# Full-height idle matmuls, a split first batch and a reordered load queue in a fused attention and SwiGLU kernel

## The chip, the cores and the metric

The kernel runs on one core of a Trainium2 chip. The metric is device time in microseconds; the median of several executions stands for a kernel. The profile is of one execution, and its own time is given beside its span.

The core's engines are named as the profile names them: PE (matmul) and PEld (its weight loads), DVE (vector), ACT (scalar), POOL (here mostly the issuer of load DMAs) and SP (the issuer of store DMAs and of DMA transposes).

## The reference

```python
batch, n_heads, seq, head_dim = (8, 12, 448, 64)
n_tokens, d_model, d_ff = (3584, 768, 1536)

scores = q @ k.T / sqrt(64)                 # per batch and head
attn = maximum(scores, 0) ** 2 / 448        # squared ReLU in place of a softmax
x = (attn @ v), heads side by side          # 3584 tokens x 768

xn = x / sqrt(mean(x * x) + 1e-6) * rms_g
out = (silu(xn @ w_gate) * (xn @ w_val)) @ w_out
```

Inputs and output are float32; inside, the kernel works in bf16 with float32 sums.

## The kernel before

**Tiling.** Heads go in pairs (six pairs, two to a "visit", so three visits to a sub-batch). Batch 0 is cut into two halves of 224 query columns, `a0` and `a1` (`subs[0]`, `subs[1]`); each later batch is one piece of 448. For each piece the kernel makes

- transposes of q and k into `qkT` (PSUM tile `psT`), by the PE for batches 0 and 1, by DMA after that;
- scores in units (`psS`, and `psR` for the last 64 keys), then ReLU and square into `r` (L656/L658 and L664), on DVE and ACT, some squares on POOL in batch 1;
- attention times v, three visits (`psAV`), copied to `xT` and squared to `x`;
- the sum of squares by a matmul against ones (`psSS`), then Ln, Exp and a table load on ACT and six scalings on DVE into `xn`;
- the feed-forward: gate (`psg`) and value (`psv`) by blocks f of 128 features, twelve in all, evacuated as `sil` on ACT and `hT` on DVE; then the output projection (`psO`), three column pieces to a tile of 128 tokens.

Most matmuls use 64 rows of the array. Two of them, one on the low and one on the high 64 rows, run side by side: the low half works one segment while the high half works the segment before it.

**The order is written out ahead of time.** The program places every instruction by hand (`tc.manual_schedule()`). While the kernel is built, the class `Planner` steps through a model of the engines: each half of the PE has a clock `t`, each other engine a time `free`, each DMA a modelled landing. At each step it picks what the model says is ready, and that fixes the order of each engine's queue. On the chip each queue then runs strictly in that order, and an instruction waits for what it really needs.

**Idle matmuls.** While batch 0's first feed-forward segment has not begun (`warm()` returns `0 not in started`), and nothing is ready in the model for 250 ns, `choose` inserts a `filler` (L293). It calls `fill()` (L1212), which issues one matmul of `ones_bf` against `busy_bf` (zeros), on the low 64 rows, 224 columns, into a free PSUM bank (`psB`, L1220). The model books 380 ns for it up to `WARM = 4500` ns and 96 ns after.

**Loads.** All are issued by POOL, in the order of L1104 to L1123, through `issue` (L405). A load waits until the one eight places before it has landed (`ahead=8`). `issue` also holds the model's price of a load on POOL (700 ns), its rate and its lag. The order is: q, k and v of batch 0 in three groups of heads (the first two query chunks of q), the other two query chunks of q, weights for blocks 0 to 8 in pairs (one `wg`, one `wv` load each), k and q of batch 1 for its first six heads, weights for blocks 8 to 12, v of batch 1, the rest of k and q of batch 1, and `wo` in two loads. For batches 2 and later, `load_later` issues loads when a batch's attention is done.

**The feed-forward's order.** `pl.stream` holds the segments. For batch 0 it has blocks 0 to 8 in pairs for `a0`, the same for `a1`, then blocks 8 to 12 one by one for `a0` and `a1` together (448 columns). The planner may take any of the first `WINDOW = 8` entries that is ready.

Of the kernel before, what the change touches and what calls it, by code (L numbers as in the profile page):

```python
# [13 lines left out]
NCH = 4  # L14
U = 7
UH = 4
# [38 lines left out]
class Planner:  # L55
# [1 line left out]


    SEM, PSUM, HAND, SW = 50.0, 210.0, 200.0, 95.0
    SLOW, WARM = 700.0, 4500.0  # L60

    def __init__(self, nc, tc, banks, wide, warm):
        self.nc, self.tc, self.banks, self.wide, self.warm = nc, tc, banks, wide, warm
# [227 lines left out]
        self.units.pop(0).begin()  # L291

    def filler(self):  # L293
        self.row()
        s = max(self.t)
        cost = self.fill() or 96.0
        TRACE.append((s, cost, "fil", "filler"))
        self.t = [s + cost, s + cost]
# [26 lines left out]
def kernel(  # L325
# [11 lines left out]
    nc = tc.nc  # L337
    P = nc.NUM_PARTITIONS
    B, H, S, D = q.shape
    T, DM = out.shape  # L340
    _, F = moe_w_gate.shape
    assert (T, DM) == (B * S, H * D) and 2 * D == P and S % NCH == 0 and B % 2 == 0 and S == U * D
    PC = S // NCH
    KT, FT, HP = DM // P, F // P, H // 2
# [29 lines left out]
    pl = Planner(nc, tc, banks, wide, None)  # L374
# [7 lines left out]
    low, high = slice(0, D), slice(D, P)  # L382
# [3 lines left out]
    ones_bf = const.tile([P, P], BF16, name="ones_bf", tag="ones_bf")  # L386
    nc.vector.memset(ones_bf[:], 1.0)
    busy_bf = const.tile([P, HALF], BF16, name="busy_bf", tag="busy_bf")
# [12 lines left out]
    ld, ldtok = {}, {}  # L401
    src_of = {"q": q, "k": k, "v": v}
    dma = {"t": 0.0, "landed": []}

    def issue(fn, nbytes, need=(), rate=385.0, cost=700.0, ahead=8):  # L405

        tok = Tok()
        land = dma["landed"]
        need = list(need) + (land[-ahead:][:1] if len(land) >= ahead else [])
        land.append(tok)  # L410

        def go(e):
            fn()
            end = pl.free["pool"]
            at = max(dma["t"], end + 1200.0)
            dma["t"] = at + nbytes / (rate if at > 8000.0 else 290.0)
            lag = 3200.0 if dma["t"] > 6000.0 else 1700.0
            TRACE.append((end - cost, dma["t"] + lag - end + cost, "dma", "%d" % nbytes))
            return dma["t"] + lag - end

        pl.task(-1, {"pool": cost}, go, need, tok)
        return tok

    def new_ld(nm, b):
        if (nm, b) not in ld:
            n, w = (PC, NCH) if nm == "q" else (P, UH)
            runs = nm == "v" or b < PE_T
            shape = [n, H, w * D] if runs else [n, w, H * D]
            ld[nm, b] = ldpool.tile(shape, BF16, name=nm + "b", tag=nm + "b")
            if nm == "k" and runs:  # L430
                nc.vector.memset(ld[nm, b][D:, :, (UH - 1) * D :], 0.0)
            ldtok[nm, b] = {}
        return ld[nm, b]

    def load_runs(nm, b, h0, h1, part, u0, u1, c0=0):

        t = new_ld(nm, b)
        n = PC if nm == "q" else D

        def go():  # L440
            nc.gpsimd.dma_start(
                out=t[part, h0:h1, c0 * D : (c0 + u1 - u0) * D],
                in_=src_of[nm][b, h0:h1].rearrange("h (p u) d -> p h (u d)", p=n)[:, :, u0 * D : u1 * D],
            )

        tok = issue(go, n * (h1 - h0) * (u1 - u0) * D * 4)
        for h in range(h0, h1):
            ldtok[nm, b].setdefault(h, []).append(tok)
        return tok

    def load_q(b, h0, h1, c0=0, c1=NCH):
        return load_runs("q", b, h0, h1, slice(0, PC), c0, c1, c0)

    def load_k(b, h0, h1):
        load_runs("k", b, h0, h1, low, 0, UH)
        load_runs("k", b, h0, h1, high, UH, U)

    def load_v(b, h0, h1):
        load_runs("v", b, h0, h1, low, 0, UH)
        load_runs("v", b, h0, h1, high, UH - 1, U)  # L460

    def load_later(b, need):

        for nm in ("k", "q"):
            t = new_ld(nm, b)
            n = PC if nm == "q" else D
            rows = src_of[nm][b].rearrange("h (p u) d -> p u h d", p=n)
            to = t[:].rearrange("p u (h d) -> p u h d", d=D)
            if nm == "q":
                parts = [(to[:], rows)]  # L470
            else:
                parts = [(to[low, u : u + 1], rows[:, u : u + 1]) for u in range(UH)]
                parts += [(to[high, u - UH : u - UH + 1], rows[:, u : u + 1]) for u in range(UH, U)]
            for o, i in parts:
                tok = issue(
                    lambda o=o, i=i: nc.gpsimd.dma_start(out=o, in_=i),  # L476
                    S * DM * 4 / len(parts), need, 200.0, 2300.0 if nm == "q" else 1080.0,
                )
                ldtok[nm, b].setdefault("all", []).append(tok)
        new_ld("v", b)  # L480
        for part, u0, u1 in ((low, 0, UH), (high, UH - 1, U)):
            def go(part=part, u0=u0, u1=u1):
                nc.gpsimd.dma_start(  # L483
                    out=ld["v", b][part, :, : (u1 - u0) * D],
                    in_=v[b].rearrange("h (p u) d -> p h (u d)", p=D)[:, :, u0 * D : u1 * D],
                )
            tok = issue(go, D * H * 4 * D * 4, need)
            for h in range(H):
                ldtok["v", b].setdefault(h, []).append(tok)

    wtok = {}

    def load_w(f0, f1):
        for nm, dst, src in (("g", wg_sb, moe_w_gate), ("v", wv_sb, moe_w_val)):
            def go(dst=dst, src=src):
                nc.gpsimd.dma_start(
                    out=dst[:, :, f0 * P : f1 * P],
                    in_=src.rearrange("(kt p) f -> p kt f", p=P)[:, :, f0 * P : f1 * P],
                )
            tok = issue(go, P * KT * (f1 - f0) * P * 4)  # L500
            for f in range(f0, f1):
                wtok[nm, f] = tok

    def load_wo(f0, f1):
        def go():
            nc.gpsimd.dma_start(
                out=wo_sb[:, f0:f1, :],
                in_=moe_w_out.rearrange("(fk p) m -> p fk m", p=P)[:, f0:f1, :],
            )
        tok = issue(go, P * (f1 - f0) * DM * 4)  # L510
        for f in range(f0, f1):
            wtok["o", f] = tok

# [355 lines left out]
    def finish(sub):  # L869

        b = sub.b
        if sub.q0 + sub.n == S and b + 2 < B:
            load_later(b + 2, [Tok(max(pl.t))])
            transpose_dma(b + 2)
# [227 lines left out]
    nc.sync.dma_start(out=g_sb[:], in_=moe_rms_g.rearrange("(kt p) -> p kt", p=P))  # L1102

    load_q(0, 0, 4, 0, 2)  # L1104
    load_k(0, 0, 4)
    identTok = pl.task(-1, {"pool": 550.0}, lambda e: masks.make_identity(nc, ident[:]) and None)
    load_q(0, 4, 8, 0, 2)
    load_k(0, 4, 8)
    load_v(0, 0, 4)
    load_q(0, 8, H, 0, 2)  # L1110
    load_k(0, 8, H)
    load_v(0, 4, H)
    load_q(0, 0, H, 2, 4)
    for f in range(0, 8, 2):
        load_w(f, f + 2)
    load_k(1, 0, H // 2)
    load_q(1, 0, H // 2)
    load_w(8, FT)
    load_v(1, 0, H)
    load_k(1, H // 2, H)  # L1120
    load_q(1, H // 2, H)
    load_wo(0, FT // 2)
    load_wo(FT // 2, FT)  # L1123


    a0, a1 = subs[0], subs[1]
# [28 lines left out]
    for si, sub in enumerate(subs):  # L1155
        lst = []
        for kk in range(HP // 2):
# [3 lines left out]
            else:  # L1161
                n = sub.n
# [25 lines left out]


    for sub in (a0, a1):  # L1190
        for f in range(0, 8, 2):
            pl.stream.append(ffn_seg([sub], "g", [f, f + 1]))
            pl.stream.append(ffn_seg([sub], "v", [f, f + 1]))
    for f in range(8, FT):
        pl.stream.append(ffn_seg([a0, a1], "g", [f]))
        pl.stream.append(ffn_seg([a0, a1], "v", [f]))
    for b in range(B):
        if b:
            for f in range(FT):
# [2 lines left out]
        full = S // P  # L1202
# [9 lines left out]
    def fill():  # L1212
        free = [x for x in wide + banks if x.free is not None and x.free <= max(pl.t)]
        if not free:
            return None
        bank = max(free, key=lambda x: x.free)
        if bank.fill is None:
            ps = bank.take("psB")
            bank.fill = ps[:, 0, :HALF] if bank in wide else ps[:, :HALF]
        nc.tensor.matmul(  # L1220
            out=bank.fill, lhsT=ones_bf[low, :], rhs=busy_bf[low, :], start=True, stop=True
        )
        cost = 96.0 if max(pl.t) > pl.WARM else 380.0
        bank.free = max(pl.t) + cost
        return cost

    def warm():
# [9 lines left out]
        return 0 not in started  # L1237

    pl.fill, pl.warm = fill, warm
    pl.run()  # L1240

# [29 lines left out]
```

## Time and profile before

| What | Value |
|---|---|
| median of 7 runs | 457.01 us (453.5 to 458.3) |
| profiled execution, its own time | 457.21 us |
| its span | 455.4 us |
| PE busy | 448.1 us, 98% of the span, 6091 matmuls |
| PEld busy | 310.0 us, 68% |
| DVE, ACT, POOL busy | 250.7, 246.3 and 86.8 us |
| granted PE clock in the profile | 0.999 |
| idle matmuls (`psB`) in the trace | 103, starting from 1.2 to 32.2 us |
| first feed-forward matmul (`psg`) | starts at 32.3 us |

Matmuls are pipelined and their ends are modelled, so the busy share of the PE does not say how full the array is: a lone 64-row matmul counts as busy while half the array is idle. The distance from one start to the next says more. A row of the timeline gives start, duration of the merged piece, engine, line, operation, output and inputs, count, and in brackets how long the engine had been idle and what ended that. In the chain of waits each row is start, length, engine, tile, line and count.

### The profile page before, as it was taken

The numbers are of one execution on the slowest core, as the hardware profiler recorded it, in microseconds if no ns is written. First come the engines' busy times: TensorE is split into PE (matmuls) and PEld (weight loads), VectorE is DVE, ScalarE is ACT, GpSimd is POOL, SyncE is SP. The second block draws the span as 40 slices with busy tenths as digits, with TensorE's granted clock in tenths as the row PEclk, the third lists the DMA queues.
The fourth block names the chain that finished last, engine by engine and source line by source line (L and its number), as shares of the span: only waits on it lengthen the run. The fifth ranks groups of instructions, "written<-read, shape, count | busy, mean of one in ns | idle before, by whom it ended". The sixth has DMA issues, their size and how long they took to land.

```text
span 455.4 us, 13555 instructions
## 1 busy us (share of the span) xinstructions
PE 448.1 (98%) x6091; PEld 310.0 (68%) x6091; DVE 250.7 (55%) x414; ACT 246.3 (54%) x363; POOL 86.8 (19%) x104
## 2 busy tenths in 40 slices
PE   8999999999999999999999999999999999999995
PEld 6777775776568666775668666775668666776784
DVE  2586978328763666367653666367653576242200
ACT  2595865527744667456654576456754566432221
POOL 8633635631134000510025000100000000000000
PEclk9999999999999999999999999999999999999999
DMA  9999997999999930699019920554002200020023
GB/s 97 187 197 203 203 179 93 173 158 195 136 78 203 176 50 2 78 189 154 1 14 195 195 53 1 68 136 96 1 1 71 73 1 1 1 71 1 1 77 99
DMA packets 133737, 44.52 MB, mean 98 GB/s; under 512 B 105712, under 2 KB 130096, under 8 KB 133680
## 3 DMA queue, kind: packets, MB, share of 16 engines
q0 software_dynamic: 94624, 24.39, 55.3%
q1 hardware_dynamic: 39056, 19.28, 23.1%
q8 instruction: 47, 0.77, 0.7%
q14 instruction: 10, 0.08, 0.1%
HBM read 48.76 MB, written 11.01 MB: 131 GB/s over the span
## 4 chain that ended last, share of the span: by engine, by line
PE 95%; DVE 3%; issue 0%; ACT 0%
PE psO L139 25%; PE psv L139 24%; PE psg L139 23%; PE psAV L820 9%; PE psS L713 6%; PE psB L1220 3%; PE psSS L139 2%; PE psT L579 2%; PE psR L734 1%; DVE r L656 1%; DVE xn L921 1%; DVE r L664 0%; DVE x L850 0%; PE psSS L947 0%; DVE qkT L594 0%
## 5 line engine op out<-in xcount | busy, mean ns | idle before, releaser
L139 PE MATMUL psv<-xn,wv_sb 64*128 64x448 bf16 (+1 forms) x1248 | 233.6, 335 | 0.3 <-DVE hT L996 0.2
L139 PE MATMUL psg<-xn,wg_sb 64*128 64x448 bf16 (+1 forms) x1248 | 233.3, 335 | 0.2
L139 PE MATMUL psO<-wo_sb,hT 64*128 64x256 bf16 x2016 | 135.5, 270 | 0.0
L139 PEld LDWEIGHTS <-wv_sb 64*128 64x128 bf16 x1248 | 104.5, 94 | 41.0 <-issue 3.4
L658 ACT ACTIVATE r<-psS 128x896 bf16<-128x896 f32 x123 | 111.3, 919 | 35.3 <-PE psS L713 33.7
L139 PEld LDWEIGHTS <-wg_sb 64*128 64x128 bf16 x1248 | 104.4, 94 | 36.6 <-issue 3.3
L139 PEld LDWEIGHTS <-hT 64*128 64x128 bf16 x2016 | 107.5, 94 | 24.1 <-issue 2.5
L664 DVE TENSOR_TENSOR r<-r 128x896 bf16<-128x896 bf16 (+1 forms) x167 | 98.9, 612 | 19.9 <-ACT r L658 19.3
L996 DVE TENSOR_TENSOR hT<-sil,psv 128x448 bf16<-128x448 bf16 x96 | 59.4, 619 | 60.8 <-PE psv L139 59.0
L983 ACT ACTIVATE sil<-psg 128x448 bf16<-128x448 f32 x96 | 52.1, 542 | 45.8 <-PE psg L139 42.7
L1073 ACT COPY ost<-psO 128x256 f32<-128x256 f32 x70 | 26.1, 372 | 66.9 <-PE psO L139 65.0
L713 PE MATMUL psS<-qkT 64*128 64x448 bf16 (+1 forms) x324 | 61.4, 338 | 0.4 <-DVE r L656 0.2
L820 PE MATMUL psAV<-r,vb 64*64 64x448 bf16 (+1 forms) x756 | 43.8, 340 | 0.4
L483 POOL DMA_DIRECT2D vb<-in_v_dram x12 | 9.5, 844 | 141.8 <-PE psO L139 141.8
L658 ACT ACTIVATE r<-psR 128x896 bf16<-128x896 f32 (+1 forms) x24 | 20.1, 839 | 29.0 <-PE psR L734 29.0
L476 POOL DMA_DIRECT2D kb<-in_k_dram x42 | 32.1, 857 | 18.9 <-DMA qb<-in_q_dram 15.9
L656 DVE TENSOR_SCALAR r<-psS 128x896 bf16<-128x896 f32 x21 | 22.9, 1089 | 23.2 <-PE psS L713 22.5
L847 DVE TENSOR_SCALAR xT<-psAV 128x896 bf16<-128x896 f32 (+1 forms) x20 | 20.9, 1045 | 24.0 <-PE psAV L820 24.0
L820 PEld LDWEIGHTS <-vb 64*64 64x64 bf16 x756 | 18.7, 107 | 20.4 <-PE psAV L820 8.7
L921 DVE SCALAR_TENSOR_TENSOR xn<-xT,g_sb,rstd 128x448 bf16<-128x448 bf16 (+1 forms) x54 | 31.0, 641 | 0.0
L713 PEld LDWEIGHTS <-qkT 64*128 64x128 bf16 x324 | 23.3, 96 | 9.1 <-issue 2.6
L1075 DVE COPY ost<-psO 128x256 f32<-128x256 f32 x14 | 5.9, 422 | 30.5 <-PE psO L139 30.5
(41 smaller groups left out, 206.5 us busy)
## 6 DMA issues: line engine op xcount, KB each, us to landing
vb<-in_v_dram POOLq DMA_DIRECT2D x14, 384.0 KB, 7.1
kb<-in_k_dram POOLq DMA_DIRECT2D x45, 96.0 KB, 8.1
qb<-in_q_dram POOLq DMA_DIRECT2D x6, 672.0 KB, 16.0
out_dram<-ost SPq DMA_DIRECT2D x8, 336.0 KB, 4.7
wo_sb<-in_moe_w_out_dram POOLq DMA_DIRECT2D x2, 1152.0 KB, 18.3
out_dram<-ost SPq DMA_DIRECT2D x8, 288.0 KB, 4.4
out_dram<-ost SPq DMA_DIRECT2D x8, 240.0 KB, 4.6
wg_sb<-in_moe_w_gate_dram POOLq DMA_DIRECT2D x4, 384.0 KB, 12.8
```

The source lines that it names most:

```text
L139: mm = self.nc.tensor.matmul(out=seg.bank["tile"][:, off : off + seg.w], lhsT=lhsT[prt], rhs=rhs[prt], start=(seg.first and h == 0 and i = ...
L476: lambda o=o, i=i: nc.gpsimd.dma_start(out=o, in_=i),
L656: nc.vector.tensor_relu(out=r[:, :, :w], in_=ps[:, :, :w])
L658: nc.scalar.activation(out=r[:, :, :w], in_=ps[:, :, :w], func=ACT.Relu)
L664: eng.tensor_tensor(out=r[:, :, :w], in0=r[:, :, :w], in1=r[:, :, :w], op=ALU.mult)
L713: nc.tensor.matmul(out=ps[:, hh, o : o + n], lhsT=t[prt, j, 0, c * P : (c + 1) * P], rhs=t[prt, j, 1, sub.q0 : sub.q0 + n], start=True, st ...
L820: mm = nc.tensor.matmul(out=ps[hh * D : (hh + 1) * D, jj, :n], lhsT=vt[prt, 2 * (ja + jj) + hh, u * D : (u + 1) * D], rhs=r[prt, hh, o : o ...
L847: nc.vector.tensor_scalar_mul(out=xT[at], in0=ps[:, :, :n], scalar1=inv_attn)
L921: nc.vector.scalar_tensor_tensor(out=xn[:, kt, q0 : q0 + n], in0=xTs[b, 0][:, kt, q0 : q0 + n], scalar=g_sb[:, kt : kt + 1], in1=rstd[:, q ...
L983: nc.scalar.activation(out=s[:, :m], in_=ps[:, :m], func=ACT.Silu)
L996: nc.vector.tensor_tensor(out=h[:, fbs[0] : fbs[-1] + 1, o : o + n], in0=s[:, :m].rearrange("p (f s) -> p f s", s=n), in1=ps[:, :m].rearra ...
L1073: nc.scalar.copy(out=ost[:, p * OW : (p + 1) * OW], in_=ps[:, :OW])
```

## The change

Five edits go together.

1. `fill()` issues its matmul on all 128 rows (`ones_bf[:]` against `busy_bf[:]`), and the model books 189 ns for it up to `WARM = 5500` ns, 96 after. `filler` treats it as an operation of mode "full", with the model's switch of 95 ns.
2. Batch 0's feed-forward goes by pairs of blocks for all twelve blocks, first in `a0`, then in `a1`.
3. k and q of batch 1 for the first six heads are issued ahead of the weights for blocks 4 to 8.
4. The model of a load is new: its POOL time depends on its number of runs, its rate on the length of a run, its lag on the time.
5. The load helpers are rearranged; they issue the same transfers.

```diff
-    SLOW, WARM = 700.0, 4500.0
+    SLOW, WARM = 700.0, 5500.0
...
     def filler(self):
-        self.row()
-        s = max(self.t)
+        s = max(self.t) + (self.SW if self.mode != "full" else 0.0)
+        self.mode = "full"
         cost = self.fill() or 96.0
...
-    def issue(fn, nbytes, need=(), rate=385.0, cost=700.0, ahead=8):
+    def issue(fn, nbytes, run, need=(), rate=None, ahead=8):
...
+        rate = rate or (385.0 if run > 512 else 280.0)
+        cost = 500.0 + 0.45 * nbytes / run
...
-            at = max(dma["t"], end + 1200.0)
-            dma["t"] = at + nbytes / (rate if at > 8000.0 else 290.0)
-            lag = 3200.0 if dma["t"] > 6000.0 else 1700.0
+            at = max(dma["t"], end + 1000.0)
+            dma["t"] = at + nbytes / rate
+            lag = 3200.0 if dma["t"] > 13000.0 else min(2500.0, max(850.0, 0.38 * dma["t"] - 575.0))
...
     load_q(0, 0, H, 2, 4)
-    for f in range(0, 8, 2):
-        load_w(f, f + 2)
+    load_w(0, 2)
+    load_w(2, 4)
     load_k(1, 0, H // 2)
     load_q(1, 0, H // 2)
+    load_w(4, 6)
+    load_w(6, 8)
     load_w(8, FT)
...
     for sub in (a0, a1):
-        for f in range(0, 8, 2):
+        for f in range(0, FT, 2):
             pl.stream.append(ffn_seg([sub], "g", [f, f + 1]))
             pl.stream.append(ffn_seg([sub], "v", [f, f + 1]))
-    for f in range(8, FT):
-        pl.stream.append(ffn_seg([a0, a1], "g", [f]))
-        pl.stream.append(ffn_seg([a0, a1], "v", [f]))
...
         nc.tensor.matmul(
-            out=bank.fill, lhsT=ones_bf[low, :], rhs=busy_bf[low, :], start=True, stop=True
+            out=bank.fill, lhsT=ones_bf[:], rhs=busy_bf[:], start=True, stop=True
         )
-        cost = 96.0 if max(pl.t) > pl.WARM else 380.0
+        cost = 96.0 if max(pl.t) > pl.WARM else 189.0
```

More of the change, by code (lines that the diff above doesn't have):

```diff
@@ L433, in new_ld, with landed, load_q, load_runs @@
         return ld[nm, b]
-    def load_runs(nm, b, h0, h1, part, u0, u1, c0=0):
-        t = new_ld(nm, b)
-        n = PC if nm == "q" else D
+    def landed(nm, b, h0, h1, tok):
+        for h in range(h0, h1):
+            ldtok[nm, b].setdefault(h, []).append(tok)
+    def load_q(b, h0, h1, c0=0, c1=NCH):
+        t = new_ld("q", b)
         def go():
             nc.gpsimd.dma_start(
-                out=t[part, h0:h1, c0 * D : (c0 + u1 - u0) * D],
-                in_=src_of[nm][b, h0:h1].rearrange("h (p u) d -> p h (u d)", p=n)[:, :, u0 * D : u1 * D],
-            )
[L446 to L452, printed above, removed]
+                out=t[:, h0:h1, c0 * D : c1 * D],
+                in_=q[b, h0:h1].rearrange("h (p u) d -> p h (u d)", p=PC)[:, :, c0 * D : c1 * D],
+            )
+        landed("q", b, h0, h1, issue(go, PC * (h1 - h0) * (c1 - c0) * D * 4, (c1 - c0) * D * 4))
+    def load_runs(nm, b, h0, h1, part, u0, u1, need=()):
+        t = new_ld(nm, b)
+        def go():
+            nc.gpsimd.dma_start(
+                out=t[part, h0:h1, : (u1 - u0) * D],
+                in_=src_of[nm][b, h0:h1].rearrange("h (p u) d -> p h (u d)", p=D)[:, :, u0 * D : u1 * D],
+            )
+        run = (u1 - u0) * D * 4
+        landed(nm, b, h0, h1, issue(go, D * (h1 - h0) * run, run, need))
     def load_k(b, h0, h1):
@@ L456, in load_k, with load_v @@
         load_runs("k", b, h0, h1, high, UH, U)
-    def load_v(b, h0, h1):
-        load_runs("v", b, h0, h1, low, 0, UH)
-        load_runs("v", b, h0, h1, high, UH - 1, U)
+    def load_v(b, h0, h1, need=()):
+        load_runs("v", b, h0, h1, low, 0, UH, need)
+        load_runs("v", b, h0, h1, high, UH - 1, U, need)
     def load_later(b, need):
@@ L476, in load_later @@
                     lambda o=o, i=i: nc.gpsimd.dma_start(out=o, in_=i),
-                    S * DM * 4 / len(parts), need, 200.0, 2300.0 if nm == "q" else 1080.0,
+                    S * DM * 4 // len(parts), D * 4, need, 200.0,
                 )
                 ldtok[nm, b].setdefault("all", []).append(tok)
[L480 to L489, printed above, removed]
+        load_v(b, 0, H, need)
     wtok = {}
@@ L499, in go @@
                 )
-            tok = issue(go, P * KT * (f1 - f0) * P * 4)
+            tok = issue(go, P * KT * (f1 - f0) * P * 4, (f1 - f0) * P * 4)
             for f in range(f0, f1):
@@ L509, in go @@
             )
-        tok = issue(go, P * (f1 - f0) * DM * 4)
+        tok = issue(go, P * (f1 - f0) * DM * 4, DM * 4)
         for f in range(f0, f1):
```

## Prediction

> **What bounds the kernel now.** I read the page's slices first, then counted work by stage, then followed the chain of waits through the first stage, then POOL's timeline for the landings.
>
> The slices say that the PE is busy throughout, and that its granted clock is full in all of them:
>
> ```profile
> PE   8999999999999999999999999999999999999995
> DVE  2586978328763666367653666367653576242200
> PEclk9999999999999999999999999999999999999999
> DMA  9999997999999930699019920554002200020023
> ```
>
> Both rows hide the loss. Busy counts idle matmuls (psB) and lone half-array matmuls as full. So I asked for the groups by form in stretches of 10 us, and gave each matmul the array time that it needs: columns / 2.4 GHz + 2.5 ns (the spacing at full speed in this trace: 224 columns start 96 ns apart), times the share of the array that its rows and columns take (a half for 64*128, a quarter for 64*64); a transpose 28 ns, psB nothing. For instance, of stretch 30 to 40:
>
> ```profile
> L139 PE MATMUL psg<-xn,wg_sb 64*128 64x224 bf16 x46 | 5.7, 257 | 0.0
> ```
>
> 46 x 95.8 / 2 = 2.2 us of array. Summed, the array's work is 419.3 us of the 455.4. The time lost runs up to 9.1 us at 10, 16.4 at 20, 21.6 at 30, 25.2 at 40, 26.7 at 50, 28.8 at 60, 30.2 at 90, and stays between 30.0 and 31.2 from there to 450. From 90 us on the array is full: what the first 60 us save arrives at the end undiminished; nothing after it can be gained.
>
> The chain of waits of that first stage (start, length, engine, tile):
>
> ```profile
> 7.87 0.19 PE psB L1220
> 8.05 1.37 PE psT L579 x24
> ...
> 12.22 2.05 PE psB L1220 x11
> 14.27 1.36 PE psT L579 x23
> 15.64 0.86 PE psB L1220 x4
> 16.49 0.94 PE psAV L820 x15
> ...
> 19.11 1.37 PE psT L579 x21
> 20.48 1.07 PE psS L713 x12
> 21.55 0.76 PE psB L1220 x8
> ...
> 24.94 0.71 PE psT L579 x24
> ```
>
> The same work costs two prices. Eleven psB take 2.05 us at 12.2 (187 ns each), eight take 0.76 at 21.55 (95 ns); 24 transposes take 1.37 us at 8.05 and 0.71 at 24.94. The array runs at half speed from the start to about 21.3 us, although the PEclk row shows nothing of it. And it does so under 36 psB back to back from 1.18 to 8.05 us.
>
> The queue is in order, and the planner booked 96 ns for psB that cost 187. So the PE falls behind its plan and real work waits behind psB. POOL's timeline shows by how much, since each load waits for the landing of the eighth before it:
>
> ```profile
> 10.79 0.94 POOL L441 DMA_DIRECT2D qb<-in_q_dram  x1 [0.40 <-DMA kb<-in_k_dram]
> 14.99 0.87 POOL L496 DMA_DIRECT2D wg_sb<-in_moe_w_gate_dram  x1
> 17.79 0.82 POOL L496 DMA_DIRECT2D wg_sb<-in_moe_w_gate_dram  x1 [1.10 <-DMA vb<-in_v_dram]
> 29.51 0.83 POOL L496 DMA_DIRECT2D wv_sb<-in_moe_w_val_dram  x1 [1.63 <-DMA wg_sb<-in_moe_w_gate_dram]
> 39.03 0.83 POOL L506 DMA_DIRECT2D wo_sb<-in_moe_w_out_dram  x1 [0.77 <-DMA qb<-in_q_dram]
> ```
>
> k of heads 4 to 8 is in at 10.8, its transposes run at 14.27. The issue at 14.99 waits for nothing, so k of heads 8 to 12 is in by then; its transposes run at 19.11. v is complete at 17.7, the gate weights of blocks 4 and 5 at 29.4, q of batch 1 at 39.0. DVE and ACT are not what holds this back before 21 us, but are nearly full after it (columns: PE, PEld, DVE, ACT, POOL):
>
> ```profile
> 16.00:21.00 5.00, 4.94 (x72) 3.21 (x72) 2.27 (x5) 2.35 (x4) 2.32 (x3) 1.00 1.56 192
> 21.00:26.00 5.00, 5.00 (x107) 4.01 (x103) 4.62 (x9) 4.82 (x8) 2.09 (x3) 1.00 1.45 197
> ```
>
> **Part 1: psB on 128 rows.** What the clock follows decides. The trace: 6.87 us of psB on half the rows did not open it; it opened at 21.3, after 16.4 to 18.7 (psAV, psR, psS on all rows) and psS from 20.4. The Trainium skill (TensorE: Matmul & The Clock Gate, Part 1: The HAM clock gate) says that one busy free-running window of about 3.4 us releases the clock, and names no number of rows. Read literally that speaks against this edit: the PE was never idle, so the clock should have opened by 8 us, rows do not matter, and the edit is worth nothing. The measured row decides: half a height, 6.87 us, not released. So I take it that rows count, and that full ones released from 1.2 us bring the clock within one to two of the page's windows, at 4.6 to 8 us (an estimate from that page; no run here shows it). No row shows a 128-row psB; the nearest is psSS, 128*128 with 224 columns, whose six matmuls take 0.68 us on the chain at 44.4: no dearer than a half-height one at full speed.
>
> What this frees on the PE up to 21.3: the real work of the chain there is psT 1.37 + 1.36 + 1.37, psS 0.37 + 0.49 + 0.19 + 0.37 + 0.49 + 1.07, psR 0.33 + 0.19, psAV 0.94 + 0.81, together 9.35 us; at full speed half of it, 4.7 us less. The 15 psB at 12.2 and 15.6 (2.9 us) shrink or go. The first transposes come when psB end: with 189 ns booked to 5.5 us and new landings, I count by hand (first q, then two k loads) a planned start of 6.4 us after about 32 psB; 6.5 to 7.1 on the chip, against 8.0, so 0.9 less. That is 8.5 us of slack, of which data allow less. The transposes of heads 8 to 12 can move from 19.1 to 15.1 at best, where their k lands: 4.0 us; they and the scores behind them then cost 1.2 us less (half of 1.37 + 1.07): 5.2. Beyond it stand DVE and ACT: visit 3 ends at 26.7, and its ReLUs and squares fill 21 to 26. Their backlog starts earlier, as they sat half idle from 8 to 21, but the two engines alternate through the same chain (ReLU 0.92 or 1.09, square 0.5, in turn). From both sides: 2.0 (only the waits up to psT at 14.3) and 5.2 us. I take 4.3, near the upper end because the pieces that the row shows late (psT, psAV) are all tied to the PE. The norm behind it (26.7 to the first psg at 32.3, 5.6 us of ACT and DVE) stays: the first psg goes to about 28.0.
>
> **Part 2: does the stage from 32 to 60 keep it?** It loses 5.8 us today (23.0 at 32.3, 28.8 at 60). It waits for a1's attention, whose q lands at 19.0 whatever is done, and for a1's xn at 51.6. Starting 4.3 us earlier could shrink or stretch this by 1.5 us; I take 0. For: a0 gets blocks 8 to 12 to work on when a1's xn is late (landed 42.5 and 46.3: issues at 27.05 and 29.51 plus the page's 15.5 and 16.8 us). Against: next part.
>
> **Part 3: the queue.** Three loads of batch 1 (192 + 144 + 336 KB) pass four of weights (384 KB each) on POOL. At the 200 GB/s of the slices, weights of blocks 4 to 8 land 3.4 us later: 32.8, 34.8, 37.4, 38.8 against 29.4, 31.4, 34.0, 35.4; k and q of batch 1 7.7 us earlier, 31.3 against 39.0. No issue is added (seven of 0.66 to 0.87 us change places), and loads behind them land as before. Blocks 4 and 5 are first used at about 41 today (their sil at 44.0, the one before at 40.9): 11 us of cover. Of that the later landing takes 3.4 and the earlier demand 4.3, so some 3.3 us are left. Cost 0; without that cover each us late is a us of waiting PE.
>
> **Part 4: blocks 8 to 12 split.** 192 matmuls of 224 columns (95.8 / 2 each, 9.20 us) for 96 of 448 (189.2 / 2, 9.08): +0.1 us. The 96 more weight loads (94 ns) hide: today's 224-column pairs start 95 ns apart. Four sil and four hT of 448 elements before and after.
>
> **Part 5: the model.** It issues nothing; load prices only move instructions. Booked landings nearer the real ones leave fewer psB in front of work, but also less reserve: a psT that runs before its load waits. Worth -0.5 to +1.5, taken as 0.
>
> **Sum.** -4.3 + 0.1 = -4.2 us on the profiled execution: 457.2 - 4.2 = 453.0. That execution stands 0.2 above the median, so 452.8.
>
> **Rivals.** *The clock does not open* (busy_bf is zeros, or something other than rows counts). For: the skill's rule, and PEclk that never moved. Against: the relation of 187 to 95 ns in equal instructions. Then only booked times change, psB booked right for 4 us: the 0.9 of the first transposes and little more, 456.0.
>
> *Evacuation takes over.* DVE and ACT at 4.6 and 4.8 of 5 us from 21 to 26 hold visit 3; only the 2 us up to psT survive: 455.0. For: that row. Against: both half idle before it.
>
> *The weights come late and the clock falls back: slower.* Once batch 0's feed-forward begins no psB are issued, so a PE that waits is really idle. It decides if demand for blocks 4 to 8 moves up more than 7.6 us (11 less 3.4), or a1's attention no longer fills the gap. One wait of 3.4 us lets the clock drop by the skill's window, and up to two more windows at half speed cost another 3.4: 6.8 - 4.2 = +2.6, 459.6. For: the four landings. Against: 3.3 us of cover, and psS and psAV of a1 to run meanwhile.
>
> *More than forecast:* k of batch 1 and blocks 8 to 12 fill the holes from 40 to 60 (3.6 us lost today); with 2 of it, 450.8, and with part 1 at its 5.2, 449.9.
>
> **How the numbers follow.** About 0.5% (2.3 us) is what a measurement of this kernel can tell from no change: below 454.7 is faster, above 459.3 slower. Forecast 0.50 and more than forecast 0.20, all faster; evacuation 0.14, a fifth of it still faster; no clock 0.08, same; late weights 0.08, nearly all slower. Faster 0.73, same 0.19, slower 0.08. The range leaves out the late weights and the far end of the large gain: 449.2 to 456.5.
>
> **What would show it.** psB 187 ns apart only up to 4.6 to 8 us, then 96; psT x24 in about 0.7 us from its first run, at 6.5 to 7.1; psT of heads 4 to 8 near 11 and of 8 to 12 near 15; psg first near 28; lost array time near 24.5 at 60 us and flat from 90. Wrong: psB still at 187 ns at 12 us; psg first after 31; PE idle before psg or psv between 32 and 42 ended by a weight DMA.

## The result and the profile after

The changed kernel takes 454.13 us (median of 17, 452.33 to 455.98) against 457.05 (median of 40): a ratio of 0.9945, 95% interval 0.9928 to 0.9963. That is 2.9 us less by the medians and 2.5 by the ratio; the forecast was 452.8. Medians and ratios, here and below, are over the executions that the record marks as fast. The profiled execution took 454.27 us with a span of 452.5.

The page's slices of the changed kernel, the same rows as before:

```profile
PE   8999799999999999999999999999999999999995
DVE  3789576418844676467643766367653566242200
PEclk9999899999999999999999999999999999999999
DMA  9999999999999910998039910645002200020023
```

In the rows of PE and PEclk one digit each is new: a 7 and an 8, in the same slice (45 to 57 us). The chain of waits of the changed kernel's first stage (start, length, engine, tile):

```profile
1.18 5.76 PE psB L1222 x30
6.94 0.86 PE psT L582 x24
...
10.11 0.77 PE psT L582 x24
10.88 0.91 PE psB L1222 x7
11.80 0.70 PE psAV L823 x16
...
25.17 0.93 ACT r L661
26.10 0.04 issue
26.14 0.37 PE psS L716 x4
26.51 0.57 PE psg L139 x6
```

The idle matmuls now cost 130 ns at 10.88 (seven in 0.91 us, with the wait behind them), not 187; the 24 transposes 0.77 us, not 1.37. The array came to full speed at about 7 us instead of 21.3. In the timeline, whose pieces overlap, the first psg starts at 26.35 us, 6.0 earlier.

The lost array time, counted as in the prediction, shows that this gain did not all last. (The price of a matmul in that count, 95.8 ns for 224 columns and 189.2 for 448, is the distance of starts at full speed: psB 95 ns apart, and psv of 448 columns at 97.74, 97.93 and 98.12 us in the kernel before.)

```
us             20     30     40     50     60     90
before       16.4   21.6   25.2   26.7   28.8   30.2
after        14.2   19.1   20.1   23.5   26.4   27.5
gain          2.2    2.5    5.1    3.2    2.4    2.7
```

5.1 us are won by 40, and 2.7 of them are given back by 60. Some stages of the changed kernel there (columns: PE, PEld, DVE, ACT and POOL busy with counts, granted clock, DMA share, GB/s):

```profile
46.00:48.00 2.00, 1.98 (x30) 1.49 (x29) 0.82 (x2) 1.97 (x3) 1.72 (x2) 1.00 1.45 196
48.00:50.00 2.00, 0.00 (x0) 0.00 (x0) 1.97 (x6) 1.97 (x2) 0.75 (x1) 1.00 1.48 200
51.00:52.00 1.00, 1.00 (x14) 0.89 (x9) 0.86 (x2) 1.00 (x3) 0.66 (x1) 0.71 1.47 201
52.00:53.00 1.00, 1.00 (x13) 0.96 (x13) 0.38 (x2) 0.72 (x1) 0.83 (x2) 0.50 1.29 204
53.00:54.00 1.00, 1.00 (x15) 1.00 (x12) 0.38 (x1) 0.00 (x0) 0.65 (x1) 0.50 1.22 211
54.00:55.00 1.00, 1.00 (x16) 0.96 (x14) 0.00 (x0) 0.28 (x1) 0.56 (x1) 0.58 1.17 217
```

From 48 to 50 the PE runs nothing; then its clock is at half for some 3.4 us. The timeline says what it waits for:

```profile
50.28 0.37 PE L716 MATMUL psS<-qkT 64*128 64x448 bf16 x2 [2.30 <-ACT r L661]
```

Scores of batch 1 stand at the head of the PE's queue and wait 2.3 us for a ReLU on ACT. And ACT, in its timeline:

```profile
44.46 1.28 ACT L986 ACT_TABLE_LOAD   x1 [0.75 <-issue]
45.76 0.54 ACT L986 ACTIVATE sil<-psg 128x448 bf16<-128x448 f32 x1
46.32 1.28 ACT L909 ACT_TABLE_LOAD   x1
47.61 0.39 ACT L909 ACTIVATE rstd<-rstd 128x224 f32<-128x224 f32 x1
48.02 1.28 ACT L912 ACT_TABLE_LOAD   x1
49.31 0.92 ACT L661 ACTIVATE r<-psS 128x896 bf16<-128x896 f32 x1
```

In a1's norm a Silu (`sil`) now stands between Ln (at 43.27, just ahead of these rows) and Exp (47.61). In the trace a table load stands ahead of the Silu and another ahead of Exp (the first two above, 2.57 us). The kernel before has neither: its groups show 18 table loads, the changed kernel's 20. Exp comes 3.9 us after Ln has ended, and the ReLU that would free a PSUM tile for the PE waits behind it all. The scalings of a1's xn on DVE, first in the chain of the kernel before and then in the timeline of the changed one:

```profile
48.55 3.04 DVE xn L921 x6
```

```profile
48.03 2.27 DVE L924 SCALAR_TENSOR_TENSOR xn<-xT,g_sb,rstd 128x224 bf16<-128x224 bf16 x6 [1.08 <-ACT rstd L909]
```

The feed-forward begins 6.0 us earlier, but a1's xn only 0.5: the PE comes early to a stage whose input is as late as before.

So two questions were left: which of the edits makes the gain, and which makes the crowd on ACT and DVE at 40 to 55 us.

### The profile page after: what moved, and what is told of

The parts are those of the page before. It is cut to its first block, busy times and chain, and to the rows that moved or that the text cites. A ratio compares the mean times of both kernels' runs of the same rounds, so it can differ in the third digit from the quotient of the medians.

```text
span 452.5 us, 13692 instructions
## 1 busy us (share of the span) xinstructions
PE 442.8 (98%) x6162; PEld 309.0 (68%) x6162; DVE 251.1 (55%) x416; ACT 246.8 (55%) x362; POOL 88.0 (19%) x105
## 4 chain that ended last, share of the span: by engine, by line
PE 94%; ACT 2%; DVE 2%; issue 1%; ACTq 0%
PE psO L139 25%; PE psv L139 25%; PE psg L139 23%; PE psAV L823 8%; PE psS L716 6%; PE psSS L139 2%; PE psB L1222 2%; PE psT L582 1%; PE psR L737 1%; DVE r L667 1%; ACT r L661 1%; ACT L912 1%; DVE xT L850 0%; ACT qkT L599 0%; DVE r L659 0%
## 5 line engine op out<-in xcount | busy, mean ns | idle before, releaser
L139 PEld LDWEIGHTS <-wv_sb 64*128 64x128 bf16 x1296 | 108.6, 95 | 39.0 <-issue 3.0
L139 PEld LDWEIGHTS <-wg_sb 64*128 64x128 bf16 x1296 | 107.9, 94 | 35.4 <-issue 2.3
L667 DVE TENSOR_TENSOR r<-r 128x896 bf16<-128x896 bf16 (+1 forms) x166 | 100.4, 623 | 20.8 <-ACT r L661 20.0
L716 PE MATMUL psS<-qkT 64*128 64x448 bf16 (+1 forms) x324 | 59.2, 329 | 3.2 <-ACT r L661 2.6
L458 POOL DMA_DIRECT2D vb<-in_v_dram x18 | 13.8, 806 | 142.2 <-PE psO L139 140.5
L661 ACT ACTIVATE r<-psR 128x896 bf16<-128x896 f32 (+1 forms) x25 | 21.4, 857 | 34.3 <-PE psR L737 34.2
L659 DVE TENSOR_SCALAR r<-psS 128x896 bf16<-128x896 f32 x22 | 23.8, 1087 | 22.3 <-PE psS L716 21.6
L850 DVE TENSOR_SCALAR xT<-psAV 128x896 bf16<-128x896 f32 (+1 forms) x22 | 22.1, 1006 | 24.7 <-PE psAV L823 24.7
L716 PEld LDWEIGHTS <-qkT 64*128 64x128 bf16 x324 | 22.3, 94 | 11.6 <-issue 4.6
```

The source lines that it names most:

```text
L139: mm = self.nc.tensor.matmul(out=seg.bank["tile"][:, off : off + seg.w], lhsT=lhsT[prt], rhs=rhs[prt], start=(seg.first and h == 0 and i = ...
L659: nc.vector.tensor_relu(out=r[:, :, :w], in_=ps[:, :, :w])
L661: nc.scalar.activation(out=r[:, :, :w], in_=ps[:, :, :w], func=ACT.Relu)
L667: eng.tensor_tensor(out=r[:, :, :w], in0=r[:, :, :w], in1=r[:, :, :w], op=ALU.mult)
L716: nc.tensor.matmul(out=ps[:, hh, o : o + n], lhsT=t[prt, j, 0, c * P : (c + 1) * P], rhs=t[prt, j, 1, sub.q0 : sub.q0 + n], start=True, st ...
L850: nc.vector.tensor_scalar_mul(out=xT[at], in0=ps[:, :, :n], scalar1=inv_attn)
```

## The experiments

The theory: rows of the array at work open the clock, which is the whole gain; the early batch-1 loads, or the new load prices, bring batch 1's scores in front of a1's norm, which gives part of it back. The rivals: the new order makes the gain and the clock is incidental; or what is lost at 48 us is lost to loads. Each run below was timed against the kernel before on the same chip; e1, e2, e3 and e5 shared one chip, e4, e6, e7 and e8 another, the rest a third. The kernel before had medians of 457.3 to 457.4 on these, so differences between runs of different chips are given by medians and by ratios where the two differ. In the diffs, `-` is the kernel that the heading names.

**e1: the changed kernel with half-height idle matmuls.**

```diff
-out=bank.fill, lhsT=ones_bf[:], rhs=busy_bf[:], ...
+out=bank.fill, lhsT=ones_bf[low, :], rhs=busy_bf[low, :], ...
```

> The changed kernel with its idle matmuls put back on 64 rows, nothing else (same order of all queues). Theory (rows release the clock): psB stay 187 ns apart and 24 psT take 1.37 us until about 18 to 21 us, the first psg comes at 30 to 32 us instead of 26.3, and the time goes back by 3 us or more, to 457 to 460. Rival (the gain is from the new order and load prices, the clock is incidental): first psg near 27, time within 1 us of 454.1.

455.51 us (median of 22), ratio 0.998 (0.9958 to 1.0001). Its profiled execution took 459.1, well above that median, so its trace is read for the clock and the first stage alone. Its chain of waits:

```profile
6.93 1.37 PE psT L582 x24
...
16.52 1.37 PE psT L582 x22
```

With the same queues, transposes cost 1.37 us at 16.5 still, and the first psg is at 30.0 instead of 26.35. The clock follows the rows. The time is another matter: it went back by 1.4 us (median) instead of the 3 or more expected. What is left of the gain, 1.9 us by the medians, is no longer clear of nothing by the interval. So inside this order the rows bring far less than the 4.9 us that e2 shows in the old one; that the crowd at 40 to 55 us takes the rest would fit, but is not shown by a typical execution of e1.

**e2: the kernel before with full-height idle matmuls.**

```diff
-out=bank.fill, lhsT=ones_bf[low, :], rhs=busy_bf[low, :], ...
+out=bank.fill, lhsT=ones_bf[:], rhs=busy_bf[:], ...
```

> The kernel before with its idle matmuls on 128 rows, nothing else (its own order, its own booked prices). Theory: psB 187 ns apart only to about 7 us, first psg at 28 to 29 us instead of 32.3, and since no Silu stands between this kernel's Ln and Exp nothing is given back: 452.5 to 454. Rival (rows alone do little without the new order): 456 to 457.

452.25 us (median of 6), ratio 0.9892 (0.9863 to 0.992). One line, with queues and booked prices as before, does more than the whole change; the intervals do not meet. The rival that needs the new order for the gain is out: the other edits together cost 1.9 us by the medians. Its a1 norm on ACT, in its timeline:

```profile
41.10 0.45 ACT L900 ACTIVATE rstd<-psSS,eps_col 128x224 f32<-128x224 f32 x1
42.14 0.92 ACT L658 ACTIVATE r<-psS 128x896 bf16<-128x896 f32 x1 [0.60 <-PE psS L713]
42.96 0.38 ACT L906 ACTIVATE rstd<-rstd 128x224 f32<-128x224 f32 x1
43.35 1.28 ACT L909 ACT_TABLE_LOAD   x1
```

No Silu inside; a1's xn starts at 43.76, 4.3 us before that of the changed kernel, although its first psg (27.75) is 1.4 later. Lost array time at 60 us: 24.5; PEclk 1.00 in every stage from 8 to 70.

**e3: the changed kernel with Ln and Exp as one task.**

```diff
         def power(e):
+            log(e)
             nc.scalar.activation(
...
-        a = pl.task(0, {"act": switch + act_cost(n, 1.03)}, log, [Tok(ready)], None, free_bank(bk["bank"]))
-        parts = [pl.task(0, {"act": act_cost(n, 1.03) + 1283.0}, power, [a])]
+        parts = [pl.task(0, {"act": switch + 2 * act_cost(n, 1.03) + 1283.0}, power,
+                         [Tok(ready)], None, free_bank(bk["bank"]))]
```

> The changed kernel with Ln and Exp of the norm emitted as one task of ACT, so that no Silu can be placed between them. Theory (the gain is given back at 44 to 55 us: two table loads of 1.28 us that only this kernel has, a PE idle for 2.3 us behind them, then 3.4 us at half clock): the two table loads go, PE idle at 48 to 50 us under 0.5 us, PEclk 1.00 throughout, lost array time at 60 us near 22.5 to 24 instead of 26.4, time 450 to 452. Rival (PE there waits for batch 1's scores or for weights, the table loads only lie beside it): 453.5 to 454.5.

452.90 us (median of 5), ratio 0.990 (0.988 to 0.9919). The two table loads are gone, the clock stays at 1.00 in its trace, lost time at 60 is 24.7. The time fell by 1.2 us in the median and by 2.0 in the ratio (0.9945 to 0.990, intervals that do not meet). That is between the two expectations (450 to 452, and 453.5 to 454.5), and the lost time missed the 22.5 to 24 expected: a1's xn now starts at 46.12 and its last three scalings at 49.81, since DVE is full (5.00 of 5 us from 40 to 45 and from 45 to 50). The table loads are one part; the crowd on DVE is another.

**e5: the changed kernel with blocks 8 to 12 unsplit.**

```diff
-        for f in range(0, FT, 2):
+        for f in range(0, 8, 2):
...
+    for f in range(8, FT):
+        pl.stream.append(ffn_seg([a0, a1], "g", [f]))
+        pl.stream.append(ffn_seg([a0, a1], "v", [f]))
```

> The changed kernel with batch 0's blocks 8 to 12 for both halves together again. Theory: the split costs 0.1 us of array and gives a0 work to do while a1's xn is missing; without it the PE has less to do at 40 to 52 us: 454 to 456, if the Silu stays between Ln and Exp. Rival (the split is what put the Silu there, by having a0's gate blocks ready at that moment): the extra table loads go and the time falls to 451 to 453.

457.89 us (median of 14), ratio 1.001 (0.9992 to 1.0027): worse than either expectation. The Silu is still between Ln and Exp, so the split did not put it there. The PE is busy 1.47 of 5 us from 45 to 50, and the clock is at 0.82, 0.50 and 0.66 in the three stages of 5 us from 45 to 60. The split, counted at +0.1 us, is what fills the wait for a1's xn: it is worth 3.8 us in this order by the medians, 3.0 by the ratios.

**e4: the changed kernel with the old load order**, and **e6: the same with blocks 8 to 12 unsplit as well** (left of the change: full rows and the new prices, of loads and of idle matmuls).

```diff
     load_w(0, 2)
     load_w(2, 4)
-    load_k(1, 0, H // 2)
-    load_q(1, 0, H // 2)
     load_w(4, 6)
     load_w(6, 8)
+    load_k(1, 0, H // 2)
+    load_q(1, 0, H // 2)
```

> The changed kernel with the load order of before (batch 1's first k and q behind the weights of blocks 4 to 8). Theory (batch 1's early k and q let its scores be placed in front of a1's norm, and their ReLUs and squares fill DVE and ACT and hold up a1's xn): with them later, a1's xn comes before 46 us instead of 48.0, no Silu between Ln and Exp, time 451.5 to 453. Rival (the new load prices alone make the crowded order): 453.5 to 455.

> The changed kernel with the load order and the feed-forward order of before: what is left of the change is full rows, the new booked price of an idle matmul and the new load prices. If the load order is what costs: as the kernel before with full rows, 452 to 453. If the new prices cost by themselves: first psg near 26.5 but the extra table loads and an idle PE at 45 to 55 us, 454 to 457.

e4: 453.15 us (median of 22), ratio 0.9939 (0.9912 to 0.9966). By the ratio that cannot be told from the changed kernel (0.9945); by the median it is 1.0 less. a1's xn starts at 44.52 instead of 48.03, as expected; yet the Silu is still between Ln and Exp, which was not. e6: 457.23 us (median of 22), ratio 1.0011 (0.9986 to 1.0037), with the Silu there too. So the new prices alone make the Silu's place, whatever the loads, and without the split they undo the whole gain of the rows. Which of the new prices does it, that of a load or that of an idle matmul, no run separates.

**e7: the kernel before with full rows and the split**, and **e8: the kernel before with full rows and the new load order** (old prices in both; each is e2 with the one further edit).

```diff
-        for f in range(0, 8, 2):                       # e7
+        for f in range(0, FT, 2):
...
-    for f in range(8, FT):
...
-    for f in range(0, 8, 2):                           # e8
-        load_w(f, f + 2)
+    load_w(0, 2)
+    load_w(2, 4)
     load_k(1, 0, H // 2)
     load_q(1, 0, H // 2)
+    load_w(4, 6)
+    load_w(6, 8)
```

> The kernel before with full rows and with batch 0's blocks 8 to 12 split, its own load order and prices. The split costs 0.1 us of array and gives work while a1's xn is missing: 451.5 to 452.5 against the 452.25 of full rows alone. If the split costs something not yet seen, 453 or more.

> The kernel before with full rows and with batch 1's first k and q ahead of the weights of blocks 4 to 8, its own prices and feed-forward order. Theory that the load order crowds DVE and ACT ahead of a1's xn: 453.5 to 457, a1's xn at 46 us or later (43.8 with full rows alone), and perhaps the extra table loads. Rival: 451.5 to 452.5.

e7: 452.41 us (median of 22, 450.37 to 457.0), ratio 0.9917 (0.989 to 0.9943): no difference from full rows alone that could be told. e8: 456.61 us (median of 22), ratio 1.0012 (0.9991 to 1.0033): the load order by itself costs 4.4 us by the medians and 5.5 by the ratios, whose intervals are far apart. Its profiled execution took 458.2. It has no Silu between Ln and Exp, so this is the other part alone. DVE in its timeline:

```profile
42.52 2.08 DVE L656 TENSOR_SCALAR r<-psS 128x896 bf16<-128x896 f32 x2
44.52 0.61 DVE L664 TENSOR_TENSOR r<-r 128x896 bf16<-128x896 bf16 x1
45.05 0.60 DVE L996 TENSOR_TENSOR hT<-sil,psv 128x448 bf16<-128x448 bf16 x1
45.58 2.06 DVE L664 TENSOR_TENSOR r<-r 128x896 bf16<-128x896 bf16 x1
47.57 1.89 DVE L921 SCALAR_TENSOR_TENSOR xn<-xT,g_sb,rstd 128x224 bf16<-128x224 bf16 x5
```

Exp starts at 45.29. Then xn waits behind a square of batch 1's scores and begins at 47.57. Ahead of it stand two of batch 1's ReLUs. The square takes 2.06 us, where one of the same size at 44.52 takes 0.61; POOL runs a square of its own beside the long one (45.49 to 47.16). And then the PE starves, and its stages show the price (columns as above):

```profile
48.00:50.00 2.00, 1.26 (x5) 0.46 (x5) 2.00 (x7) 1.15 (x2) 0.75 (x1) 0.96 1.48 199
50.00:52.00 2.00, 1.59 (x10) 1.25 (x11) 1.42 (x3) 0.00 (x0) 1.13 (x2) 0.50 1.48 195
55.00:56.00 1.00, 1.00 (x15) 1.00 (x12) 0.00 (x0) 0.07 (x1) 0.00 (x0) 0.50 1.16 212
56.00:57.00 1.00, 1.00 (x18) 0.96 (x15) 0.17 (x1) 0.00 (x0) 0.00 (x0) 0.67 1.15 209
```

The clock is at half from about 49.8 to 56.7, for 6.8 us. From 52 on the PE is busy all the time, and DVE and ACT have almost nothing to do (0.2 and 0.6 of 5 us). Half of 6.8, or 3.4 us of array, is lost, most of it after the data have come.

**e9: e7 with Ln and Exp as one task**, and **e13: e4 with Ln and Exp as one task** (the edit of e3).

```diff
-        parts = [pl.task(0, {"act": act_cost(n, 1.03) + 1283.0}, power, [a])]
+        parts = [pl.task(0, {"act": switch + 2 * act_cost(n, 1.03) + 1283.0}, power, ...)]
```

> The kernel before with full rows, the split, and Ln and Exp of the norm as one task of ACT (loads and prices of before). There Ln and Exp already stand next to each other but for one ReLU of 0.92 us, so a1's xn could come up to 0.9 us earlier: 451 to 452 if that still holds the PE at 45 to 50 us; the same 452.4 if DVE, which scales xn and squares the scores, is what holds it.

> The changed kernel with the load order of before and with Ln and Exp as one task. If load order and extra table loads are the two costs and add up: 2.5 us of ACT less ahead of a1's xn, no half-clock stretch at 45 to 55 us, 450.5 to 452 (453.15 with the old load order alone). If the table loads only lie beside a DVE that is late anyway: 453.

e9: 453.52 us (median of 6), ratio 0.992 (0.989 to 0.9951): no gain. Exp now ends at 41.26, but xn starts at 43.09 (43.19 in e7), behind a ReLU on DVE. One of its six scalings then takes 2.05 us instead of 0.44, while POOL runs a square (43.55 to 45.24). e13: 452.57 us (median of 5), ratio 0.9895 (0.9866 to 0.9925), PEclk 1.00 throughout. By the intervals that is just faster than the changed kernel (whose interval begins at 0.9928), though on five executions and another chip; it cannot be told from full rows alone. Against e4 it is 0.6 us lower in the median and 2.0 in the ratio, with intervals that overlap; the sum that was expected is not clearly there.

**e12 and e14: the changed kernel with idle matmuls on 96 rows, and on 128 rows but 64 columns.** One execution of each.

```diff
-out=bank.fill, lhsT=ones_bf[:], rhs=busy_bf[:], ...
+out=bank.fill, lhsT=ones_bf[:96, :], rhs=busy_bf[:96, :], ...          # e12
+out=bank.fill[:64], lhsT=ones_bf[:, :64], rhs=busy_bf[:], ...          # e14
```

> The changed kernel with its idle matmuls on 96 of the 128 rows; the order of all queues is the same. If the clock follows the share of rows at work and the limit lies between 64 and 96: psB 96 ns apart from about 7 us as with 128 rows. If it needs the full height: 187 ns until about 18 us, as with 64 rows.

> The changed kernel with its idle matmuls on 128 rows but only 64 of the 128 columns. If the clock follows rows: psB 96 ns apart from about 7 us. If it follows the share of the array at work: as with 64 rows, 187 ns until about 18 us.

455.07 and 455.32 us. The PE in the timeline, e12 first, then e14:

```profile
3.75 2.28 PE L1222 MATMUL psB<-busy_bf,ones_bf 96*128 96x224 bf16 x16
6.48 0.41 PE L582 MATMUL psT<-ident,kb 128*64 128x128 bf16 x8 [0.45 <-DMA kb<-in_k_dram]
```

```profile
3.74 2.37 PE L1222 MATMUL psB<-busy_bf,ones_bf 128*64 128x224 bf16 x16
6.46 0.41 PE L582 MATMUL psT<-ident,kb 128*64 128x128 bf16 x8 [0.35 <-DMA kb<-in_k_dram]
```

Sixteen in 2.3 us, about 140 ns on average: the clock opened among them, at some 5 us. 96 rows suffice. And 128 rows by 64 columns open it, while 64 rows by 128 columns, the same half of the array, do not in 6.87 us (kernel before) or 5.75 us (e1): it is rows that count. Where between 64 and 96 the limit lies was not tried.

The factors side by side, all with full rows (medians in us; the kernel before 457.0 to 457.4 beside them):

```
                                  unsplit        split
old prices, old load order        452.25 (e2)    452.41 (e7)
old prices, new load order        456.61 (e8)    not run
new prices, old load order        457.23 (e6)    453.15 (e4)
new prices, new load order        457.89 (e5)    454.13 (the change)
```

## Why the prediction was right, and where

The way and most of the size came from the term that was argued, the clock. That 454.1 lies as near to 452.8 as it does is in part luck: the first psg came 1.7 us earlier than forecast, and the stage after it lost 3.4 us more than before, where the sum had 0.

**Part 1, the clock: right in kind, too small.** The measured row (6.87 us of half-height work not released) was the better guide than the rule that the prediction cites, which names no rows; e1, e2 and e14 show it. The first psg was put at 28.0 and came at 26.35, 6.0 us gained and not 4.3. The term that was too small is the landing of k for heads 8 to 12: an issue that waited for nothing at 14.99 says only "landed by then", and I used it as the landing. The transposes of those heads ran at 13.7 in the changed kernel, 5.4 us earlier than before, where I had allowed 4.0 as the most that was possible. First transposes: forecast 6.5 to 7.1, measured 6.9. Taken alone the edit is worth 4.9 us of 457.4 (e2; 3.7 to 6.3 by its interval), against 4.3 in the sum.

**Part 2, "I take 0": wrong.** Lost time at 60 us was put near 24.5 and is 26.4. From the first psg to 60 the kernel before loses 5.0 us (from 23.8 at 32.31, counted again to the start of psg; the prediction had 23.0), the changed one 8.4 (from 18.0 at 26.35). I had put the difference within 1.5 of 0. What failed is that a1's xn did not move up with the first psg (48.03 against 48.55), so the PE ran out of work that it could start.

**Part 3, "cost 0": wrong, though its own numbers were right.** The landings were forecast at 32.8, 34.8 and 37.4 us for the weights and 31.3 for q of batch 1. POOL's timeline of the changed kernel, where each load waits for the eighth before it:

```profile
32.03 0.76 POOL L458 DMA_DIRECT2D vb<-in_v_dram  x1 [1.66 <-DMA qb<-in_q_dram]
33.28 0.66 POOL L458 DMA_DIRECT2D kb<-in_k_dram  x1 [0.50 <-DMA wg_sb<-in_moe_w_gate_dram]
35.28 0.66 POOL L458 DMA_DIRECT2D kb<-in_k_dram  x1 [1.34 <-DMA wv_sb<-in_moe_w_val_dram]
37.27 0.77 POOL L446 DMA_DIRECT2D qb<-in_q_dram  x1 [1.34 <-DMA wg_sb<-in_moe_w_gate_dram]
```

They are 32.0, 33.3, 35.3 and 37.3, and no psg or psv waited for a weight between 32 and 42. I asked only what would come too late. The cost is in what comes early. With k and q of batch 1 in sooner, its scores are placed sooner, and their ReLUs and squares take DVE and ACT ahead of a1's xn. With the old prices that costs 4.4 us (e2 to e8). The new prices crowd the same place already; there it costs 0.7 and 1.0 by the medians (e6 to e5, and e4 to the change), which the intervals do not tell from nothing.

**Part 4, the split.** +0.1 us of array fits (e2 to e7 shows no difference), but "work when a1's xn is late" was only named in part 2 and given no size. Where xn is late it is worth 3.8 and 4.1 us by the medians (e5 to the change, e6 to e4), 3.0 and 3.3 by the ratios.

**Part 5, prices "taken as 0", -0.5 to +1.5.** Between e2 and e6 they cost 5.0 us, between e7 and e4, with the split, 0.7, which the intervals do not tell from nothing. They issue nothing, but they put the Silu between Ln and Exp.

**The slower rival** named the right end (a PE without work whose clock falls back once psB are no longer issued) and the wrong cause (late weights). It happened at half the price that it gave the clock: 1.7 us of array, as the sum of the stages gives it (0.29 + 0.50 + 0.50 + 0.42 for 51 to 55 us), behind a wait of 2.3 us instead of 3.4. So 454.1 is a gain of 5.1 us at 40 us, less 2.4 by 90, in terms that the sum had at 0.

Left open: six of the 40 timed runs of the kernel before lie between 453.5 and 453.9 us and none between that and 456.6. That would fit a clock that opens earlier in some executions, but no such execution was traced. The group's share differs: 6 of 35 beside e1, e2, e3 and e5, 16 of 65 beside e4, e6, e7 and e8, none of 11 beside e9 and e13. It moves the ratios, so e13's are the least comparable with the others. What the extra table loads cost alone is known only roughly: 0.6 to 1.2 us by the medians of e13 and e3, 2.0 by their ratios.

The half clock's own price was not tried apart from the wait that causes it: a filler there needs a free PSUM tile, which is what the PE waits for. The executions of the changed kernel order themselves by the mean clock that was granted, though: three with 0.991 took 455.4 to 456.0 us, fourteen with 0.993 to 0.996 took 453.8 to 454.9, and one with 0.998 took 452.33. Steps of about 1.6 us fit 3.4 us more or less at half clock (1.7 us of array), but the wait may differ with it.

## What to carry to other kernels

Count the array's work by stage (columns, rows, share of the array) before trusting a busy PE or a granted clock of 1.00: equal instructions at 187 and 95 ns showed a cold array that neither row did. Open its clock with idle matmuls on more than 64 rows; 96 and 128 did it here. When a schedule is written out ahead of time, ask of each load moved forward not only what it delays but which work it lets in front of the critical step, and keep operations that run without a table load between them in one task. Try the edits one by one as well: here one line of the five edits, alone, did more than all of them.

## What the hardware showed that was not expected

Idle matmuls of 64 rows by 128 columns left the clock at half until 19 us (e1) and 21 us (the kernel before). Those of 96 by 128 and 128 by 64 opened it at 5 us, those of 128 by 128 at 4 to 7 us in ten traces (in e5 seven psB start between 2 and 3 us and 13 between 4 and 5). It is the rows at work that count, not the share of the array, and zeros as the moving data do not prevent it.

The clock falls back without a long silence. In the changed kernel it fell at 51.4, after 2.3 us of idle PE (48.0 to 50.3), and in e4 at 47.7, after 1.6 us (45.2 to 46.8): both times some 1 us after the PE had work again. In e8 it fell at 49.8, after idle times of at most 0.75 us, while the PE ran five matmuls from 48.0 to 49.8. The Trainium skill (TensorE: Matmul & The Clock Gate, Part 1: The HAM clock gate) gives one idle window of about 3.4 us. In none of these three did the PE stand idle that long; a window with little in it would explain all three, but how little is not shown. The length fits: the clock was at half for 3.4 us in the changed kernel, 6.8 in e8 and 10.2 in e5, one, two and three windows.

A square on POOL and an instruction of DVE beside it go together with a longer DVE instruction: 2.06 us instead of 0.61 in e8, 2.05 instead of 0.44 in e9. What they share the traces do not show.

The PEclk row shows these drops (0.50) but not the cold start: it reads 1.00 from the start of the profile, in every run.
